# A fused attention and feed-forward kernel: 13 score groups a batch, a ring of exponentials, and one fixed order of all operations

## The chip, the cores and the metric

The kernel runs on one core of one Trainium2 chip. The metric is the time that one execution takes on the device, in microseconds (us); a kernel is run several times and the median is given. TensorE (PE in the profile) does matrix products and transposes, VectorE (DVE) and ScalarE (ACT) do the elementwise work, GpSimd (POOL) and SyncE (SP) mostly start transfers (DMA) here. PSUM is the memory that the results of TensorE go to. An execution is called slow when it lies over 1.5% above the fastest one of the same kernel; verdicts use the fast executions alone.

## The reference

Eight batches of causal attention with 8 heads, 576 queries of 64 numbers and 16 extra keys that every query sees; then three products without a nonlinearity over all 4608 tokens.

```python
k_all = concat([beacon_k, k]); v_all = concat([beacon_v, v])   # 592 keys
scores = q @ k_all.T / sqrt(64)          # causal mask, beacons always seen
a = exp(scores - max); a /= a.sum()
x = (a @ v_all) -> [4608, 512]           # tokens x (heads * 64)
h = (x @ w1) * (x @ w2) @ w3             # 512 -> 1024 -> 1024
out = h @ w_out                          # 1024 -> 512, float32
```

Since nothing stands between w3 and w_out, both kernels multiply the two weights once (Wt = w3 w_out) and use the product. Queries and keys are small, so neither kernel subtracts the maximum.

## The kernel before

It alternates "steps" of attention (64 of them, two to a pair of heads) with matmuls taken from a generator of the feed-forward part. The parts that the change and the argument touch:

```python
GROUPS = [                       # one pair of heads: 4 groups of 368 to 512 columns
    [(1, 112, 128, 0), (0, 0, 240, 128)],
    [(0, 240, 256, 0), (1, 240, 256, 256)], ...]
def scores(s):                   # two 64-row matmuls side by side, one a head
    for g in (2 * half, 2 * half + 1):
        ps = psS.tile([P, 2, 512], FP32, name="ps")        # 2 such pairs in PSUM
        for jt, q0, n, col in GROUPS[g]:
            for hh in range(2):
                nc.tensor.matmul(ps[:, hh, ds(col, n)],
                    kT[ds(hh * 64, 64), t, ts(jt, P)], qT[ds(hh * 64, 64), t, ds(q0, n)])
...
def ff_out(mc, gT):
    ...
        nc.vector.tensor_scalar(ot, pm, float(1.0 / GS), None, ALU.mult)
        nc.sync.dma_start(out[ds(mc * 512 + mt * P, P), :], ot)   # all 36 stores on SyncE
def transpose_qk(b, c):                                           # batches 2 to 7
    nc.sync.dma_start_transpose(qTs[i][:, :, ds(c * P, rows)], q16s[i][:rows, c, :])
    nc.sync.dma_start_transpose(kTs[i][:, :, ds(c * P, P)], k16s[i][:, c, :])
...
def stream():                    # the feed-forward generator
    for mc in range(2): gTs.append((yield from ff_ab(mc)))
    yield from fuse()            # w3 transposed and multiplied by w_out: after two chunks
    ...
for s in range(NSB, NS):         # main loop, from batch 1
    scores(s + 1); exps(s + 1, 0); values(s); emit_ff(k1)
    exps(s + 1, 1); mask(s + 1, 0); emit_ff(fill[s] - k1); mask(s + 1, 1)
    ...
```

The queries and keys of batches 0 and 1 come in large pieces, are cast by VectorE and transposed on TensorE; those of later batches are loaded by GpSimd in pieces of 64 numbers and transposed by DMA from SyncE's queue. So is the attention output x of those batches (x of batches 0 and 1 is transposed on TensorE).

The softmax here doesn't subtract the row's maximum and nothing guards it: scores larger than these inputs give would overflow.

Of the kernel before, what the change touches and what calls it, by code (L numbers as in the profile page):

```python
# [17 lines left out]
GROUPS = [  # L18
    [(1, 112, 128, 0), (0, 0, 240, 128)],
    [(0, 240, 256, 0), (1, 240, 256, 256)],  # L20
    [(3, 368, 128, 0), (2, 240, 256, 128)],
    [(4, 496, 80, 0), (3, 496, 80, 80), (2, 496, 80, 160), (1, 496, 80, 240), (0, 496, 80, 320)],
]
GW = [368, 512, 384, 400]
GO = [400, 768, 1280, 0]
PW = 1664

QT0 = [0, 112, 240, 368, 496]
QTN = [112, 128, 128, 128, 80]
BLK = [  # L30
    [(0, GO[0] + 128)],
    [(0, GO[0] + 240), (1, GO[0])],
    [(0, GO[1]), (1, GO[1] + 256), (2, GO[2] + 128)],
    [(0, GO[1] + 128), (1, GO[1] + 384), (2, GO[2] + 256), (3, GO[2])],
    [(4, 0), (3, 80), (2, 160), (1, 240), (0, 320)],
]
# [3 lines left out]
def kernel(  # L40
# [27 lines left out]
    VS = 72  # L68
    scale = float(D**-0.5)
# [11 lines left out]
    MA = const.tile([P, 240], FP16, name="MA")  # L81
    MB = const.tile([P, 256], FP16, name="MB")
    ident = const.tile([P, P], FP16, name="ident")

    ptp = ctx.enter_context(tc.tile_pool(name="ptp", bufs=2))
    xp = ctx.enter_context(tc.tile_pool(name="xp", bufs=2))
    sm = ctx.enter_context(tc.tile_pool(name="sm", bufs=4))
    gp = ctx.enter_context(tc.tile_pool(name="gp", bufs=2))
    wp = ctx.enter_context(tc.tile_pool(name="wp", bufs=2))
    early = ctx.enter_context(tc.tile_pool(name="early", bufs=8))  # L90
    tiny = ctx.enter_context(tc.tile_pool(name="tiny", bufs=2))
    bkp = ctx.enter_context(tc.tile_pool(name="bkp", bufs=1))
    asb = ctx.enter_context(tc.tile_pool(name="asb", bufs=2))
    op = ctx.enter_context(tc.tile_pool(name="op", bufs=3))
    psS = ctx.enter_context(tc.tile_pool(name="psS", bufs=2, space=bass.MemoryType.PSUM))
    psV = ctx.enter_context(tc.tile_pool(name="psV", bufs=1, space=bass.MemoryType.PSUM))
    psM = ctx.enter_context(tc.tile_pool(name="psM", bufs=3, space=bass.MemoryType.PSUM))

    ctx.enter_context(tc.manual_schedule())


    def load_q(b, c):
        rows = min(P, S - c * P)
        nc.gpsimd.dma_start(  # L104
            q16s[b % NB2][:rows, c, :].rearrange("s (h d) -> s h d", h=H),
            q[b, :, ds(c * P, rows), :].rearrange("h s d -> s h d"),
        )

    def load_kv(b, jt, src, beacon, dst):
        p0 = Nb if jt == 0 else 0  # L110
        s0 = max(0, jt * P - Nb)
        rows = min(P - p0, S - s0)
        nc.gpsimd.dma_start(  # L113
            dst[ds(p0, rows)], src[b, :, ds(s0, rows), :].rearrange("h s d -> s h d")
        )
        if jt == 0:
            nc.gpsimd.dma_start(dst[0:Nb], beacon[b].rearrange("h n d -> n h d"))

    def load_k(b, jt):
        load_kv(b, jt, k, beacon_k, k16s[b % NB2][:, jt, :].rearrange("s (h d) -> s h d", h=H))  # L120

    def load_v(b, jt):
        load_kv(b, jt, v, beacon_v, vas[b % NB2][:, jt, :, 0:64])

    def transpose_qk(b, c):
        i = b % NB2
        rows = min(P, S - c * P)
        nc.sync.dma_start_transpose(qTs[i][:, :, ds(c * P, rows)], q16s[i][:rows, c, :])
        nc.sync.dma_start_transpose(kTs[i][:, :, ds(c * P, P)], k16s[i][:, c, :])


    early_qk, early_b = {}, {}

    def load_pair(b, t):
        for i, src in enumerate((q, k)):
            st = early.tile([P, 2, RUN * D], FP32, name="st")
            if b:
                nc.vector.memset(st[0:1, 0, 0:1], 0.0)
            nc.sync.dma_start(
                st[:NR], src[b, ds(2 * t, 2)].rearrange("h (p j) d -> p h (j d)", j=RUN)  # L140
            )
            early_qk[b, t, i] = st
        if t == 0:
            bst = bkp.tile([Nb, H, D], FP32, name="bst")
            nc.sync.dma_start(bst, beacon_k[b].rearrange("h n d -> n h d"))
            early_b[b] = bst

    o16s = {}

    def cast_pair(b, t):  # L150
        if t == 0:
            b16 = bkp.tile([Nb, DM], FP16, name="b16")
            nc.vector.tensor_copy(b16, early_b[b].rearrange("p h d -> p (h d)"))
            early_b[b] = b16
        o16s[t] = []
        for i in range(2):
            o16 = tiny.tile([P, RUN, P], FP16, name=f"o16_{i}")
            nc.vector.tensor_copy(  # L158
                o16[:NR].rearrange("p j (h d) -> p h j d", h=2),
                early_qk[b, t, i][:NR].rearrange("p h (j d) -> p h j d", j=RUN),  # L160
            )
            o16s[t].append(o16)

    def pe_transpose_pair(b, t):
        qT, kT = qTs[b % NB2], kTs[b % NB2]
        for o16, dst, off, copy in (
            (o16s[t][0], qT, 0, nc.vector.tensor_copy if b or t != 1 else nc.scalar.copy),
            (o16s[t][1], kT, Nb, nc.scalar.copy),
        ):
            pt = psM.tile([P, 1024], FP16, name="pm")  # L170
            for j in range(RUN):
                nc.tensor.transpose(pt[:, ds(j * NR, NR)], o16[:NR, j, :], ident[:NR, :NR])  # L172
            if off:
                nc.tensor.transpose(
                    pt[:, ds(S, Nb)], early_b[b][:, ts(t, P)], ident[:Nb, :Nb]
                )
                copy(dst[:, t, 0:Nb], pt[:, ds(S, Nb)])
            copy(  # L178
                dst[:, t, ds(off, S)].rearrange("p (i j) -> p i j", j=RUN),
                pt[:, 0:S].rearrange("p (j i) -> p i j", j=RUN),  # L180
            )

    def pe_transpose_x(b):
        for i in range(NJT):
            pt = psM.tile([P, NT, P], FP16, name="pm")
            n = QTN[i]
            for t in range(NT):
                nc.tensor.transpose(
                    pt[:, t, 0:n], x16s[b][:n, i, ts(t, P)], ident[:n, :n]
                )  # L190
            dst = xT[:, :, ds(b * S + QT0[i], n)]
            if i % 2:
                nc.scalar.copy(dst, pt[:, :, 0:n])
            else:
                nc.vector.tensor_copy(dst, pt[:, :, 0:n])


    zeros = const.tile([P, 512], FP16, name="zeros")
    nc.vector.memset(zeros, 0.0)  # L199

    def spin(n):
        pm = psM.tile([P, 512], FP32, name="pm")
        for _ in range(n):
            nc.tensor.matmul(pm, zeros[:, 0:P], zeros)  # L204

    nc.vector.memset(ident, 1.0)
    nc.vector.memset(MA, 1.0)
    nc.vector.memset(MB, 1.0)

    def constants(i):  # L210
        nc.vector.memset(kTs[i][:, :, ds(S + Nb, NJT * P - S - Nb)], 0.0)
        nc.vector.memset(vas[i][64:128, 4, :, :], 0.0)
        nc.vector.memset(vas[i][:, 0:4, :, 64:65], 1.0)
        nc.vector.memset(vas[i][0 : S + Nb - 4 * P, 4, :, 64:65], 1.0)

    constants(0)

    for t in range(NT):
        load_pair(0, t)
    nc.gpsimd.affine_select(  # L220
        ident,
        ident,
        pattern=[[1, P]],
        compare_op=ALU.is_equal,
        fill=0.0,
        base=0,
        channel_multiplier=-1,
    )
    for m, base in (
        (MA[:, 0:128], 0),  # L230
        (MA[:, 128:240], Nb),
        (MB[:, 0:128], 0),
        (MB[:, 128:256], 0),
    ):
        nc.gpsimd.affine_select(
            m,
            m,
            pattern=[[1, m.shape[1]]],
            compare_op=ALU.is_ge,
            fill=0.0,  # L240
            base=base,
            channel_multiplier=-1,
        )
    for c in range(NJT):
        load_v(0, c)
    for i in range(NB2):
        nc.gpsimd.memset(k16s[i][64:128, 4, :], 0.0)
        nc.gpsimd.memset(q16s[i][64:128, 4, :], 0.0)
    for c in range(4):
        for i, w in enumerate((moe_w1, moe_w2)):  # L250
            nc.gpsimd.dma_start(
                w12[:, :, ds(i * DF + c * 256, 256)],
                w[:, ts(c, 256)].rearrange("(t p) f -> p t f", p=P),
            )

    def fuse():
        def w3_transposed(kt):
            pt = psM.tile([P, NFT, P], FP16, name="pm")
            for rt in range(NFT):
                nc.tensor.transpose(pt[:, rt, :], w316[:, kt // 2, kt % 2, ts(rt, P)], ident)  # L260
# [295 lines left out]
```

## Time and profile before

| | before |
|---|---|
| time, median of the first 3 runs | 322.3 us (319.26 to 323.62) |
| span of the profiled execution | 316.5 us |
| PE busy | 294.4 us, 93% |
| work of PE at full pace (worked out in the prediction) | 261 us |
| DVE, ACT, POOL busy | 167.1, 158.1, 110.9 us |
| DMA packets under 512 B | 143,104 of 156,960 |

The main lines of the profile stand in the prediction. Two things that the prediction left aside turned out to matter. The first is how long the first pieces of q and k take to land (the view of DMA issues; columns: out<-in, queue, kind, count, KB of one, median us from issue to landing):

```profile
st<-in_q_dram SPq DMA_DIRECT2D x8, 288.0 KB, 7.0
st<-in_k_dram SPq DMA_DIRECT2D x8, 288.0 KB, 7.9
```

The second is what SyncE's queue waits for (the view of that queue's waits; us in total, times, longest):

```profile
SPq L323 <- DVE ot L322: 54.8, 14, 15.1
SPq L323 <- DVE pT L384: 40.0, 10, 15.4
SPq L128 <- DMA q<-in_q_dram: 38.3, 2, 21.7
```

L323 is the output store, and it stands in the same queue as the transposes of q, k and x. The queue takes its entries in order, so while a store waits for a copy, no transpose behind it can start. I had read these lines as harmless, since a queue that waits is not an engine that waits.

### The profile page before, as it was taken

What the parts mean: (1) busy time and instruction counts of PE and PEld (TensorE: products, weight loads), DVE (VectorE), ACT (ScalarE), POOL (GpSimd) and SP (SyncE); (2) the same over time, 40 slices, a digit from 0 to 9 for tenths busy, and PEclk for the clock granted to TensorE, in tenths of its full rate; (3) what the DMA queues carried; (4) which work ended last, traced back from release to release, by engine and by line L of the source; (5) the groups of instructions that cost most, each with busy time, mean ns of one, the idle gap of its engine ahead of it and who ended that gap; (6) DMA issues with size and microseconds to landing.
All of it is one profiled execution on the core that took longest, in us unless ns stands there. A gap on an engine that the chain in (4) does not pass through costs nothing.

```text
span 316.5 us, 7016 instructions
## 1 busy us (share of the span) xinstructions
PE 294.4 (93%) x2826; PEld 151.3 (48%) x2826; DVE 167.1 (53%) x391; ACT 158.1 (50%) x230; POOL 110.9 (35%) x147
## 2 busy tenths in 40 slices
PE   8877688899989999999999999999999999999995
PEld 3445254454545554455544455445554544444442
DVE  4767277455554445555555565555555634344342
ACT  1983466666636554376546645654665231230320
POOL 8954686347756680384067305000000000000000
PEclk9999899999999999999999999999999999999999
DMA  8999999999999999999989999935600330202003
GB/s 188 207 230 284 163 133 143 181 210 175 147 137 152 152 173 189 195 169 175 169 141 126 152 177 169 147 64 133 134 2 33 104 73 35 99 0 99 35 0 133
DMA packets 156960, 42.97 MB, mean 136 GB/s; under 512 B 143104, under 2 KB 151296, under 8 KB 156928
## 3 DMA queue, kind: packets, MB, share of 16 engines
q0 software_dynamic: 102240, 17.28, 75.1%
q1 hardware_dynamic: 54688, 25.25, 42.2%
q8 instruction: 22, 0.36, 0.5%
q14 instruction: 10, 0.08, 0.1%
HBM read 39.32 MB, written 9.44 MB: 154 GB/s over the span
## 4 chain that ended last, share of the span: by engine, by line
PE 78%; DMA 10%; ACT 5%; POOL 4%; DVE 2%; issue 1%; SPq 0%; DVEq 0%
PE pm L291 36%; PE pm L312 18%; PE pv L401 10%; PE ps L363 8%; DMA va<-in_v_dram 5%; PE pm L269 5%; ACT pT L372 2%; DMA qT<-q 2%; DMA w<-in_moe_w_dram 2%; POOL va L113 2%; ACT a_sb L302 2%; PE pm L260 1%; DVE gT L304 1%; ACT kT L178 1%; PE pm L172 1%
## 5 line engine op out<-in xcount | busy, mean ns | idle before, releaser
L291 PE MATMUL pm<-xT,w 128*128 128x512 f16 x576 | 132.6, 382 | 0.0
L372 ACT ACTIVATE pT<-ps 128x736 f16<-128x736 f32 (+3 forms) x128 | 107.0, 869 | 39.2 <-PE ps L363 38.8
L291 PEld LDWEIGHTS <-w 128*128 128x128 f16 x576 | 54.1, 98 | 60.3 <-issue 1.4
L302 ACT ACTIVATE a_sb<-pm 128x512 f32<-128x512 f32 x72 | 43.0, 597 | 79.8 <-PE pm L291 78.8
L304 DVE TENSOR_TENSOR gT<-pm,a_sb 128x512 f16<-128x512 f32 x72 | 49.7, 690 | 46.6 <-PE pm L291 46.1
L312 PE MATMUL pm<-Wt,gT 128*128 128x512 f16 x288 | 65.9, 379 | 0.0
L113 POOL DMA_DIRECT2D va<-in_v_dram x40 | 35.7, 904 | 51.2 <-PE pv L401 27.8
L401 PE MATMUL pv<-va,pT 128*128 128x65 f16 x960 | 40.7, 194 | 5.4 <-DVE x L410 2.2
L363 PE MATMUL ps<-qT,kT 64*128 64x80 f16 (+3 forms) x704 | 37.1, 228 | 7.7 <-ACT pT L372 4.1
L409 DVE RECIPROCAL rd<-pv 128x4 f32<-128x4 f32 x64 | 12.1, 189 | 56.2 <-PE pv L401 56.2
L312 PEld LDWEIGHTS <-gT 128*128 128x128 f16 x288 | 27.1, 98 | 30.4
L401 PEld LDWEIGHTS <-pT 128*128 128x128 f16 x960 | 33.2, 97 | 15.3 <-issue 6.3
L322 DVE TENSOR_SCALAR ot<-pm 128x512 f32<-128x512 f32 x36 | 24.8, 690 | 27.7 <-PE pm L312 24.3
L363 PEld LDWEIGHTS <-kT 64*128 64x128 f16 x704 | 20.7, 94 | 34.2 <-issue 29.9
L410 DVE TENSOR_TENSOR x<-pv,rd 128x256 f16<-128x256 f32 x64 | 31.4, 490 | 2.3
L113 POOL DMA_DIRECT2D k<-in_k_dram x30 | 25.5, 850 | 10.9 <-DMA va<-in_v_dram 5.0
L104 POOL DMA_DIRECT2D q<-in_q_dram x30 | 25.7, 857 | 9.2 <-DMA va<-in_v_dram 2.7
L384 DVE TENSOR_TENSOR pT<-pT,MB 128x512 f16<-128x512 f16 x64 | 19.4, 323 | 0.0
L269 PE MATMUL pm<-wo,wT 128*128 128x512 f16 x64 | 16.4, 380 | 1.0 <-DVE wT L262 1.0
L384 DVE TENSOR_TENSOR pT<-pT,MA 128x480 f16<-128x480 f16 x32 | 12.8, 400 | 0.9 <-ACT pT L372 0.8
L204 PE MATMUL pm<-zeros 128*128 128x512 f16 x26 | 10.0, 492 | 1.3 <-DVE zeros L199 1.3
L158 DVE CAST o<-st 96x768 f16<-96x768 f32 x16 | 10.1, 660 | 1.5 <-DMA st<-in_k_dram 1.2
(43 smaller groups left out, 95.2 us busy)
## 6 DMA issues: line engine op xcount, KB each, us to landing
out_dram<-ot SPq DMA_DIRECT2D x36, 256.0 KB, 2.6
va<-in_v_dram POOLq DMA_DIRECT2D x24, 128.0 KB, 9.0
q<-in_q_dram POOLq DMA_DIRECT2D x24, 128.0 KB, 8.1
st<-in_q_dram SPq DMA_DIRECT2D x8, 288.0 KB, 7.0
st<-in_k_dram SPq DMA_DIRECT2D x8, 288.0 KB, 7.9
k<-in_k_dram POOLq DMA_DIRECT2D x18, 128.0 KB, 9.1
w<-in_moe_w_dram POOLq DMA_DIRECT2D x8, 256.0 KB, 11.0
xT<-in_moe_w_dram POOLq DMA_DIRECT2D x8, 256.0 KB, 10.4
```

Source lines behind the costliest of these rows:

```text
L104: nc.gpsimd.dma_start(q16s[b % NB2][:rows, c, :].rearrange("s (h d) -> s h d", h=H), q[b, :, ds(c * P, rows), :].rearrange("h s d -> s h d"),)
L113: nc.gpsimd.dma_start(dst[ds(p0, rows)], src[b, :, ds(s0, rows), :].rearrange("h s d -> s h d"))
L269: nc.tensor.matmul(pm, wT[:, rt, :], wo16[:, rt, :], start=(rt == 0), stop=(rt == NFT - 1),)
L291: nc.tensor.matmul(pm, w12[:, kt, ds(i * DF + kf * P, P)], xT[:, kt, ds(mc * 512, 512)], start=(kt == 0), stop=(kt == NKT - 1),)
L302: nc.scalar.activation(a_sb, pm, AF.Copy, scale=GS)
L304: nc.vector.tensor_tensor(gT[:, kf, :], pm, a_sb, ALU.mult)
L312: nc.tensor.matmul(pm, gT[:, kf, ts(mt, P)], Wt[:, kf, :], start=(kf == 0), stop=(kf == NFT - 1),)
L363: nc.tensor.matmul(ps[:, hh, ds(col, n)], kT[ds(hh * 64, 64), t, ts(jt, P)], qT[ds(hh * 64, 64), t, ds(q0, n)],)
L372: nc.scalar.activation(pT[:, :, ds(GO[g], GW[g])], pss[s][j][:, :, 0 : GW[g]], AF.Exp, scale=scale)
L384: nc.vector.tensor_tensor(blk, blk, m.unsqueeze(1).to_broadcast([P, 2, n]), ALU.mult)
L401: nc.tensor.matmul(pv[:, 2 * n + hh, 0:65], pT[:, hh, ds(col, P)], va[:, jt, 2 * t + hh, 0:65], start=(jn == 0), stop=(jn == len(BLK[i]) - 1),
L410: nc.vector.tensor_tensor(x16[:, ds(tiles[0], ni), ds(t * P, P)].rearrange("p i (h d) -> p i h d", h=2), pv[:, 0 : 2 * ni, 0:64].rearrange ...
```

## The change

The author's intent: scores in 13 full groups of 512 columns a batch, exponentials in a ring of eight group buffers, value products in two halves a pair of heads, and every operation of every engine placed by one list that was computed beforehand. In the list, `s b g n` is group g of scores of batch b into bank n, `exp`, `m`, `v`, `n` its exponential, mask, value products and division; `lq lk lv` are loads, `Dq Dk TX` DMA transposes, `l3 lo t3 e3 f ew` the product of w3 and w_out, `a b ea eb o eo st` the feed-forward part. The last letter of `st` is the queue of the output store: P is GpSimd, S is SyncE. The list is some 120 lines long; the core of the diff:

```diff
-GROUPS = [ ... ]                        # 4 groups a pair of heads, 368 to 512 columns
+def make_groups(): ...                  # 13 groups a batch, 512 columns each
+ORDER = """
+consts 0; l3 0; lq 0 0; consts 1; spin 10 7; consts 3; lo 0; lk 0 0; lkb 0; l3 1; lq 0 1; lo 1;
+lk 0 1; l3 2; lq 0 2; lo 2; lk 0 2; lq 0 3; consts 2; l3 3; lo 3; lk 0 3; cast 0 0 q; l3 4;
+tq 0 0 6; t3 0 7; eq 0 0 A 6; e3 0 D 7; lq 1 0; castb 0; cast 0 0 k; l3 5; lk 1 0; tk 0 0 5;
+...
+o 0 0 5; ea 1 0 A 6; lq 3 1; o 0 1 6; eo 0 0 A 5; lk 3 1; s 2 0 0;
+s 2 1 2; s 2 2 4; st 0 0 P; eo 0 1 A 6; exp 2 0 0; ...
+"""
-    ptp = ... bufs=2   # pT: [P, 2, 1664]          psS bufs=2, psV bufs=1, psM bufs=3
+    NRING = 8; ring = const.tile([P, NRING, 2, GP], FP16, name="ring")
+    tiles = {0: pair, 6: one_6, 7: one_7}   # banks 2-3 and 4-5: a pair, or two single banks
+    def exp(b, g, n):
+        nc.scalar.activation(held(b, g)[:, :, 0:GW], shape(n, "pair"), AF.Exp, scale=scale)
+    def st(mc, mt, e):
+        queue = nc.gpsimd if e == "P" else nc.sync
+        queue.dma_start(out[ds(mc * 512 + mt * P, P), :], st_of((mc, mt))[:, 0:DM])
-    (generators, main loop)
+    for op in ORDER: ...
```

By the list w3 and w_out are loaded first and multiplied during the start; 28 of 36 output copies go to ScalarE, and 28 of 36 output stores to GpSimd's queue; the filler matmuls at the start fall from 26 to 10.

## The prediction

> **What bounds the kernel now.** I read the page first, then the busy time in stretches of 8 us, the chain that ended last, and the waits.
>
> ```profile
> PE 294.4 (93%) x2826; PEld 151.3 (48%) x2826; DVE 167.1 (53%) x391; ACT 158.1 (50%) x230; POOL 110.9 (35%) x147
> ...
> PE   8877688899989999999999999999999999999995
> ...
> DMA  8999999999999999999989999935600330202003
> ```
>
> TensorE (PE) is the bound, and the other compute engines have room. But the busy share of PE includes the latency of each matmul, so I ask how much of the span its work needs at full pace. The end of the chain gives the pace:
>
> ```profile
> 264.46 6.91 PE pm L312 x32
> 271.37 13.81 PE pm L291 x64
> 285.18 6.91 PE pm L312 x32
> ```
>
> 13.81 us for 64 is 0.216 us for a 512-column matmul, with no hole. The same pace (columns by 2.4 per ns, plus 2.5 ns) for all that PE must do: 864 feed-forward matmuls 186.5 us; the product of w3 and w_out 64 x 0.216 + 64 transposes x 0.056 = 17.4; 960 value products of 65 columns x 0.0296 = 28.4; scores 53,248 columns for two heads side by side, 22.4; transposes of q, k and x 6.4. Sum 261. The span is 316.5; the last matmul starts some 4 us before its end. So 51 us are lost on PE. Where?
>
> ```profile
> 16.00:24.00 8.00, 5.70 (x109) 3.74 (x109) 5.34 (x27) 6.73 (x10) 4.06 (x7) 1.00 1.35 232
> ...
> 32.00:40.00 8.00, 5.15 (x40) 2.46 (x39) 2.19 (x6) 3.18 (x5) 5.47 (x7) 0.80 2.17 157
> ...
> 256.00:264.00 8.00, 8.00 (x39) 3.63 (x37) 3.39 (x5) 2.75 (x5) 0.00 (x0) 1.00 0.05 11
> ```
>
> The columns are PE, weight loads, DVE, ACT, POOL, granted clock, DMA share, GB/s. In the last line PE is full; early on it isn't, while DMA is. The chain says why:
>
> ```profile
> 12.87 7.62 DMA w<-in_moe_w_dram
> 20.77 15.64 DMA va<-in_v_dram
> 36.70 2.79 PE pm L291 x7
> ```
>
> The start waits for loads until 36.7 us. By then PE has done the attention of batch 0 (6.4 us), the q and k transposes of batch 0 and a quarter of batch 1's (2.7), the x transposes of batch 0 (1.0) and a few others (1.3): 11.3 us. So 25 us are lost before 36.7, and 26 after. Of those 26 the waits show the main part:
>
> ```profile
> ACT pT L372 <- PE ps L363: 38.8, 35, 2.5
> PEld L363 <- issue: 29.9, 69, 0.9
> ...
> PE ps L363 <- ACT pT L372: 4.1, 12, 0.6
> ```
>
> At each of 64 runs of score matmuls the weight load of keys stands idle some 0.42 us. From start to start, a matmul before a run of scores takes 0.10 us more than its columns, and the last of a run before the value products 0.18: 0.28 a run, some 13 us in the 48 runs or so after 36.7. Waits of scores for ACT to empty PSUM, and PE transposes that wait for their copies in batch 1, make up most of the rest.
>
> **What the Trainium skill says.** "TensorE: Matmul & The Clock Gate", section "Back-to-back issue gap", gives N/2.4 + 2.5 ns for a warm clock; the trace agrees (216 ns at 512), and not with the 131 ns that the section gives for real streams. The same page, "The mechanism", says that a weight load overlaps matmuls in flight only when their row groups differ. Scores use two 64-row tiles and all else 128 rows; the 0.28 us a run fits that. "What's actually happening" there says that an idle PE falls to half clock; the trace has 0.80 in 32 to 40 us, where PE idled. "DMA: Bandwidth & Descriptors", "Specifications", puts line rate at 512 B and more: here 143,104 of 156,960 packets are smaller, and while loads and DMA transposes run they move at most some 9,000 to 10,000 in 10 us (counted in the packet records).
>
> **The change, part by part.**
>
> *Scores.* 13 groups of 512 columns x 8 batches replace 128 groups of 736 to 1024 elements: the same columns, so PE work stays. ACT: 104 x 1.023 us = 106.4 for 32 x (1.023 + 0.845 + 0.820 + 0.787) = 111.2; 5 us less, off the path. Three PSUM pairs instead of two let two or three groups run together: counting the order, there are 42 runs of scores, some 33 of them after batch 1's values begin, instead of about 48. At 0.28 us that saves 4 us, and most of the 4.1 us of waits for ACT may go.
>
> *Values, masks, outputs.* The values stay 960 matmuls and 64 halves. Masks: 64 with 384 or 768 elements for 96; with some 0.14 us fixed from the rows (160 elements 232 ns, 512 elements 414 ns) about 5 us less on DVE. 28 of 36 output copies and 54 of 72 a_sb copies are on ACT, which comes to some 170 us busy, DVE to some 157. Neither bounds.
>
> *The early order.* This is the large part. w3 and w_out come first, so the 17.4 us of their product, and all q and k transposes of batch 1, fill the start. In the order, PE has 35.7 us of work ahead of the first value products of batch 1 instead of 11.3. But the loads ahead of that point grow too, by w3 and w_out: 6.3 MB read. The eight pieces of w3 landed 1.25 us apart in the trace before (67.0, 68.2, 69.5 us and on), so 10 us, and w_out takes about 5. So v of batch 1, which landed at 38.4, should land at about 52. Those first value products need all five pieces of v. PE's lag there: 52 - 35.7 = 16 us, for 25 before. Gain 9.
>
> *Rest.* Lost after that point: 33 runs x 0.28 = 9; waits for PSUM, the x transposes of batch 1 and a cold clock after the wait 5; late loads 4. That is 18 for 26. Gain 8. The 26 filler matmuls (spins) shrink to 10, in time that waits anyway.
>
> Sum: 261 + 16 + 18 + 4 (tail) = 299 us of span. The median time lies 5.8 above the profiled span (322.3 to 316.5), which gives 305; I lean to 302, because the author could place every operation where the waits allow, and I may have put the late loads and small waits too high.
>
> **Rivals.** (1) *DMA becomes the bound.* A batch has 14,080 small load packets, 7,200 of transposes and some 1,500 others: 22,800, or about 24.5 us at the best rate seen. The order gives PE 22.2 to 25.4 us of work a batch, against a measured 29 us or so now. For it: DMA is at 9 until 180 us. Against: the load queue now idles 12 to 15 us three times (waiting for value buffers), so there is slack. If it loses 3 us in each of six batches, the time is some 315. (2) *The start gains more.* If loads reach the rate that w3 had alone (0.5 MB in 1.25 us), v lands at 46 and the time is near 294. (3) *The w3 product is hidden anyway:* v of batch 1 lands at 60 and the lag stays 25; then only the 8 us of the rest are gained, 311. (4) *A fixed order is brittle:* in-order engines wait for one late copy; six score groups and few PSUM banks then cost some 0.3 us at a time. That is within the range.
>
> **Range and chances.** The start is good to 6 us, DMA to 10 on the slow side, the small waits to 5: 288 to 314. Faster by over 2% means under 315.9, and of the rivals only DMA reaches that: 0.89. Same 0.08, slower 0.03.
>
> **What would show it.** Right: feed-forward starts at about 42 us with the w3 product before it; the first value products of batch 1 near 52 wait for DMA of v; the stretches from 60 to 220 us have PE full with DMA still at 9; pure feed-forward, with no attention, fills the last 69 us (it was 61); busy ACT near 170. Wrong: waits of score matmuls for the DMA transposes of qT or kT in each batch (rival 1), v of batch 1 landing well before 48 or after 57, or ACT, not PE, ending the chain in the attention stage.

## The result

The changed kernel is correct and took 310.05 us (307.89 to 310.8, 4 runs) against 321.21 (319.26 to 323.62, 4 runs) of the kernel before. The ratio is 0.9656, with a 95% interval of 0.958 to 0.973. A ratio here is the mean time of one kernel's fast runs over that of the other's in the same rounds, so not quite the ratio of the medians that are quoted. A second measurement of the unaltered kernel in a later call gave 308.74 us and 0.9643. It is faster by some 11 us; I had predicted 302, within 288 to 314.

The page of the changed kernel, busy times and slices (a digit is the busy share of a fortieth of the span in tenths; PEclk is the granted clock, the share of its full clock at which TensorE may run):

```profile
PE 285.5 (93%) x2842; PEld 152.8 (50%) x2842; DVE 152.8 (50%) x344; ACT 163.1 (53%) x214; POOL 122.2 (40%) x170
...
PE   6697998999999695999999899999999999999994
...
PEclk9999999999999997999999999999999999999999
DMA  7999999999999999998999999999202501202103
```

PE again has holes at the start, and it has new ones in slices 14 and 16 (100 to 108 and 116 to 123 us), which the kernel before did not have. Four stretches of 8 us (columns: PE, weight loads, DVE, ACT, POOL, granted clock, DMA share, GB/s; the DMA share adds up the times of all packets over 16 engines and passes 1 where packets overlap):

```profile
24.00:32.00 8.00, 5.74 (x51) 2.98 (x48) 3.80 (x8) 4.32 (x9) 3.86 (x5) 1.00 1.17 267
...
96.00:104.00 8.00, 5.37 (x55) 2.66 (x53) 4.21 (x9) 3.53 (x5) 3.79 (x5) 1.00 2.00 127
112.00:120.00 8.00, 4.22 (x81) 2.92 (x76) 2.73 (x7) 5.97 (x7) 5.69 (x8) 0.98 2.24 212
120.00:128.00 8.00, 8.00 (x90) 4.77 (x89) 5.61 (x14) 2.54 (x3) 5.08 (x7) 0.81 1.88 150
```

In two of them PE stands for a third to half of the time while the DMA engines are full. The timeline of PE says what it waited for (start, us, operation; in brackets the idle time before it and what ended it):

```profile
104.30 0.35 PE L449 MATMUL pair<-qT,kT 64*128 64x80 f16 x10 [2.93 <-DMA kT<-k]
...
119.80 1.86 PE L521 MATMUL one<-xT,w 128*128 128x512 f16 x4 [3.78 <-DMA xT<-x]
```

Both are DMA transposes that came late. From start to start of the matmuls in the trace's records, less the time that the columns need at the pace of 216 ns for 512, I count six such holes after 100 us: 3.11, 3.96, 0.49, 0.96, 1.12 and 0.56 us, together 10.2 us. The unaltered kernel's second profile has other ones (3.35, 2.67, 0.64, 0.53), together 7.2 us: where they fall varies, that they fall doesn't. A stall can also cost after its end: the granted clock of TensorE stood at 0.5 for 3.4 us from 119.7 us (the 0.81 in the last of the four stretches), and the matmuls of that time took 1.6 us more than at full pace.

At the start the trace shows that v of batch 1 had landed at 53.4 us, as predicted (52). But its first value products began at 57.8 and did not wait for it:

```profile
52.63 5.35 PE L521 MATMUL one<-xT,w 128*128 128x512 f16 x24
57.82 0.53 PE L480 MATMUL one<-va,ring 128*128 128x65 f16 x12
```

The second line has no bracket: no idle time before it. PE was simply behind: the order puts 35.7 us of work ahead of this point, so PE was 57.8 - 35.7 = 22.1 us late. Summed over the matmul records in the same way, PE's lag (the time less the work done) was 10.5 us at 12 us, 13.9 at 20 us and 18.6 at 34 us; in the kernel before it was 9.9, 14.3 and 21.9 at these times. So 14 of the 22 us are lost in the first 20 us, with the old order as with the new one. And the first pieces of q and k land later than before (view of DMA issues, and two lines of the timeline):

```profile
st<-in_q_dram SPq DMA_DIRECT2D x8, 288.0 KB, 13.0
st<-in_k_dram SPq DMA_DIRECT2D x8, 288.0 KB, 13.5
```

```profile
10.27 0.66 PE L391 MATMUL one<-ident,o16k 96*128 96x96 f16 x6 [1.58 <-DVE o16k L383]
...
28.63 0.43 PE L391 MATMUL one<-ident,o16q 96*128 96x96 f16 x6 [1.31 <-DVE o16q L383]
```

In the two lines of the timeline PE waits for o16, the casts of such pieces on VectorE. The last piece of batch 0's k landed at 19.6 us; before it was 13.6. They share the bandwidth with w3 and w_out, 254 to 267 GB/s in these stretches.

The chain that ended last (start, us, what) points there too: where before it went through w1/w2 and v at the start, it now goes through the first piece of w3 (landed at 7.6 us) and then through a piece of q; its end is feed-forward at full pace, as before.

```profile
16.01 15.60 DMA st<-in_q_dram
...
263.85 13.81 PE one L521 x64
277.66 6.91 PE one L542 x32
```

The balance of the two spans: 316.5 - 308.5 = 8.0 us. At the first value products of batch 1 the lag was 36.7 - 11.3 = 25.4 before and is 22.1 after, so by this cut some 3 us come from the start and 5 from what follows.

The cut matters, because the two kernels reach those products at different times and with different work behind them. At equal times the matmul records say something else: at 60 us PE of the changed kernel had done 37.3 us of work against 27.8, a lead of 9.5 us; at 100 us the lead was 13.7, at 124 us, after the two large holes, 5.9, and at the end 8.4. From 60 us on the changed kernel lost 20.1 us and the kernel before 19.0. In this, holes over 0.4 us made up 10.7 for 7.1 us, the slow clock 1.6 for 0, and all that is smaller 7.8 for 11.9; the last is where fewer runs of scores should show. So by this cut the lead is won in the first 60 us, with the early order; after that, what fewer runs seem to give is taken away again by late transposes. (This rests on one profile of each kernel.) The rest of the 11 us is not in the traces: a timed execution takes 1.7 us more than its profiled span (310.18 for 308.5), so the profiled execution of the kernel before took some 318.2, which is below all three of its first timed runs. It was one of its fastest.

SyncE's and GpSimd's queues have changed places:

```profile
SPq L555 <- ACT st L292: 61.2, 8, 39.1
SPq L413 <- DMA q<-in_q_dram: 44.1, 4, 31.9
```

```profile
POOL out_dram L555 <- ACT st L292: 61.9, 19, 25.6
POOL out_dram L555 <- DVE rd L491: 23.6, 6, 9.9
```

On SyncE the 8 store waits are those of the tail, with no transposes behind them; the 28 early ones now stand on GpSimd's queue, 17 of them with loads behind them.

### The profile page after: what moved, and what is told of

Read it like the earlier page. It is cut to its first block, busy times and chain, and to the rows that moved or that the text cites. A ratio compares the mean times of both kernels' runs of the same rounds, so it can differ in the third digit from the quotient of the medians.

```text
span 308.5 us, 7036 instructions
## 1 busy us (share of the span) xinstructions
PE 285.5 (93%) x2842; PEld 152.8 (50%) x2842; DVE 152.8 (50%) x344; ACT 163.1 (53%) x214; POOL 122.2 (40%) x170
## 4 chain that ended last, share of the span: by engine, by line
PE 48%; DMA 22%; issue 14%; POOL 10%; DVE 3%; ACT 2%; POOLq 0%; SPq 0%; DVEq 0%; ACTq 0%
PE one L521 24%; PE one L542 12%; DMA va<-in_v_dram 5%; DMA st<-in_q_dram 5%; PE one L480 4%; PE pair L449 3%; DMA k<-in_k_dram 3%; POOL q L315 3%; PE one L434 3%; DMA xT<-x 2%; POOL k L323 2%; POOL out_dram L555 2%; DMA xT<-in_moe_w_dram 2%; DMA qT<-q 2%; POOL va L323 2%
## 5 line engine op out<-in xcount | busy, mean ns | idle before, releaser
L521 PE MATMUL one<-xT,w 128*128 128x512 f16 x576 | 133.3, 381 | 4.8 <-DMA xT<-x 4.7
L459 ACT ACTIVATE ring<-pair 128x1024 f16<-128x1024 f32 x104 | 98.9, 1030 | 22.5 <-PE pair L449 22.5
L536 DVE TENSOR_TENSOR gT<-one,asb 128x512 f16<-128x512 f32 x72 | 49.7, 691 | 73.3 <-PE one L521 73.3
L542 PE MATMUL one<-Wt,gT 128*128 128x512 f16 x288 | 65.3, 379 | 0.3 <-ACT ring L459 0.2
L292 ACT ACTIVATE asb<-one 128x512 f32<-128x512 f32 x54 | 32.3, 597 | 62.2 <-PE one L521 58.7
L480 PEld LDWEIGHTS <-ring 128*128 128x128 f16 x960 | 34.8, 98 | 11.0 <-issue 3.4
L480 PE MATMUL one<-va,ring 128*128 128x65 f16 x960 | 37.8, 194 | 0.4 <-ACT ring L459 0.3
L449 PE MATMUL pair<-qT,kT 64*128 64x80 f16 (+4 forms) x736 | 32.4, 228 | 5.5 <-DMA kT<-k 3.3
L292 ACT ACTIVATE st<-one 128x512 f32<-128x512 f32 x28 | 16.7, 597 | 37.0 <-PE one L542 37.0
L492 DVE TENSOR_TENSOR x<-one,rd 128x256 f16<-128x256 f32 (+1 forms) x64 | 31.4, 491 | 2.2
L469 DVE TENSOR_TENSOR ring<-ring,MX 128x384 f16<-128x384 f16 x32 | 11.3, 353 | 16.0 <-ACT ring L459 15.9
L469 DVE TENSOR_TENSOR ring<-ring,MD 128x768 f16<-128x768 f16 x32 | 17.6, 550 | 1.8 <-ACT ring L459 1.8
```

Source lines behind the costliest of these rows:

```text
L292: nc.scalar.activation(dst, src, AF.Copy, scale=by)
L449: nc.tensor.matmul(shape(n, "pair")[:, hh, ds(col, w)], kT[ds(hh * 64, 64), t, ts(jt, P)], qT[ds(hh * 64, 64), t, ds(q0, w)],)
L459: nc.scalar.activation(held(b, g)[:, :, 0:GW], shape(n, "pair"), AF.Exp, scale=scale)
L469: nc.vector.tensor_tensor(blk, blk, msk, ALU.mult)
L480: nc.tensor.matmul(pv[:, 2 * at + hh, 0 : D + 1], held(b, g)[:, hh, ds(col, P)], va[:, jt, 2 * t + hh, 0 : D + 1], start=(jt == 0), stop=( ...
L492: nc.vector.tensor_tensor(x16s[b % NB2][:, ds(2 * h, ni), ts(t, P)].rearrange("p i (h d) -> p i h d", h=2), pv[:, 0 : 2 * ni, 0:D].rearran ...
```

## The experiments

My theory after the comparison: (A) less is won at the start because PE follows a chain of pieces, casts, transposes and copies, not v of batch 1; (B) what is won afterwards comes from fewer runs of scores; (C) it is held down by DMA transposes that land late because so many small packets are in flight. Rivals: that the start is limited by the bytes ahead of v; that a change between scores and other matmuls costs nothing by itself and the cost was the wait of weights; that the order of the queues, not the packets, sets when transposes land. Twelve kernels ran, all changed from the changed kernel. The last column is the difference of the ratio to the changed kernel's 0.965 (mean of its two measurements) times 320.5 us; the intervals of two such ratios together leave it uncertain by some 3 us.

| run | median us | ratio to before, 95% | against changed, us |
|---|---|---|---|
| product_late | 313.45 | 0.977 (0.971 to 0.984) | +3.9 |
| switch_each | 317.79 | 0.993 (0.988 to 0.998) | +9.0 |
| same_rows_each | 309.53 | 0.967 (0.962 to 0.972) | +0.7 |
| no_v_after_1 (wrong on purpose) | 304.06 | 0.951 (0.946 to 0.955) | -4.6 |
| w3_one_piece (wrong on purpose) | 304.13 | 0.951 (0.947 to 0.956) | -4.4 |
| batch2_early | 318.62 | 0.995 (0.986 to 1.004) | +9.6 |
| outs_sp | 322.26 | 1.005 (0.996 to 1.014) | +12.8 |
| keys_before_w3 | 308.35 | 0.962 (0.955 to 0.969) | -1.0 |
| after_again (unaltered) | 308.74 | 0.964 (0.959 to 0.970) | -0.2 |
| outs_act | 337.04 | 1.051 (1.045 to 1.057) | +27.5 |
| outs_act_keys | 336.95 | 1.054 (1.047 to 1.060) | +28.4 |
| outs_later | 314.94 | 0.980 (0.975 to 0.985) | +4.8 |

**product_late**: the product of w3 and w_out goes behind the attention of batch 1.

```diff
-l3 0..7, lo 0..3 first; t3, e3, f, ew among the work of batch 0
+l3 0..7, lo 0..3 after "lk 2 4"; t3, e3, f, ew of all r before "o 0 0 5"
-        flat = q16s[i // 2][...]         # wT borrowed the buffers of q
+        return wTs[i]                    # own buffers
```

> The product of w3 and w_out goes back behind batch 1 (its loads after q and k of batch 2), all else as in the changed kernel (308.5 us span, 310 us median, 0.9656 of before). If filling the start with it was what gained (my prediction: PE had 9 us less lag at the first value products of batch 1), PE has 17.4 us less to do in a start that still waits, and the span rises by 8 to 14 us, to some 318, near the time of before. If the loads up to the last batch set the pace wherever the product stands, v of batch 1 lands at about 38 to 40 instead of 53 us, the product is done later in time that would have been lost to late transposes, and the span changes by less than 4 us.

It is 3.9 us slower. Its profile fell in a slow execution (314.9 us of span, mean clock 0.946), so I take only the ratio as firm. That profile has v of batch 1 landed at 41.4 us and its first value products at 45.5; with 17.4 us of product still to do, that compares with 62.9 us for the changed kernel's 57.8. So filling the start with the product is worth some 4 us of time (by the intervals, 1 to 7), not the 9 that my prediction gave to the start. The run moves the product alone; what the early q and k transposes of batch 1 are worth was not tested.

**switch_each** puts a tiny matmul over all 128 rows in front of each of the 104 score groups; **same_rows_each** is its control, the same matmul over 64 rows.

```diff
 def s(b, g, n):
+    nc.tensor.matmul(shape(n, "pair")[:, 0, 0:16], zeros[:, 0:P], zeros[:, 0:16])
 # control: zeros[0:64, 0:P], zeros[0:64, 0:16]
```

> One tiny matmul of 128 rows ahead of each of the 104 score groups, so that every group, and not only each of the 42 runs of groups, leaves and enters the 64-row tiles. By the prediction's 0.28 us a run (0.10 in, 0.18 out) 62 more switches cost some 12 us of PE time (62 x 0.2, as the way out to the next group's own loads is shorter) plus 104 x 0.03 = 3: span 318 to 326 if PE sets the pace, some 3 to 6 us if half of it disappears in waits for DMA. If a switch costs nothing and the idle weight load is only waiting that lies elsewhere, the span rises by 3 us or less.

> The control of the run with 128 rows: the same 104 tiny matmuls, but of 64 rows like the scores, so no switch between tile shapes is added. If the switch costs (8.8 us more than the changed kernel was the whole), this one costs 104 x 0.03 = 3 us or less, 1 us after what waits absorb. If it is any added weight load and matmul that costs, it is as slow as that run: 7 to 9 us more.

The 128-row matmul costs 9.0 us and the 64-row one nothing that can be measured (0.7, inside the intervals). So it is the change of rows, not the number of matmuls. The list has 42 runs of scores; 104 need 62 changes more each way. From start to start the trace of switch_each shows 0.093 us over the columns for a change out of scores and 0.107 for one into them (medians), 62 x 0.20 = 12 us gross, of which 9 arrive at the end: PE then waits less for late transposes (holes over 0.4 us after 60 us: 4.2 us for 10.7). Net, that is 9.0 / 62 = 0.145 us a run. The change has 22 runs fewer than the kernel before (42 for 64), so that part is worth some 3.2 us net (an estimate from this run).

**no_v_after_1** does not load v after batch 1, **w3_one_piece** loads only the first of eight pieces of w3. Both give wrong results on purpose; they take bytes and packets away without moving anything.

```diff
 def lv(b, c):
+    if b > 1: return          # and in lvb       (no_v_after_1)
 def l3(r):
+    if r: return              # t3 reads piece 0 each time   (w3_one_piece)
```

> Wrong result on purpose: v of batches 2 to 7 is not loaded (batches 0 and 1 are used again), 28,400 of 154,000 packets less, no instruction of a compute engine less. If the rate of small packets makes the transposes of q, k and x late, the six stalls of PE after 100 us (3.1 + 4.0 + 0.5 + 1.0 + 1.1 + 0.6 = 10 us) and the slow clock after the second go, and the span falls to 296 to 300. If the stalls come from the order in which the transposes are issued behind each other, they stay: 305 or more.

> Wrong result on purpose: one of the eight pieces of w3 is loaded and used eight times, 3.7 MB of 11 MB less to read by 32 us, the same work on every compute engine. If the bytes read set the pace of the start (some 370 GB/s), v of batch 1 lands at about 43 instead of 53 us, the lag of PE by 60 us falls from 22.6 to some 14, and the span falls by 8 to 12 us, to about 298, as all later loads come 10 us sooner too. If the chains of small copies and transposes set the start, the lag falls by less than 3 us, though the later loads still come sooner: 303 to 307.

Without v the time falls by 4.6 us. The large holes at 101 and 116 us are gone, but the scores still wait once for queries at 127.4 to 130.1 (2.67 us). So these loads do make transposes late, and removing them wins about half of the 10 us. Whether by their packets or by their place in GpSimd's queue the run can't say, since it removes both. For w3 it is the same gain, and for a reason that I had not seen: v of batch 1 landed at 46.5, seven us sooner, and PE came to its value products at 56.3 for 57.8, only 1.5 sooner. The landing of v doesn't set the start. Nor does that of q and k explain it alone: their pieces also came faster than in the changed kernel,

```profile
st<-in_q_dram SPq DMA_DIRECT2D x8, 288.0 KB, 9.5
```

and the last one at 30.5 us instead of 35.3, but its transpose started at 37.1 instead of 38.5. (The first eight landed at nearly the same times in both, until 18.6 and 19.6 us, so the run says nothing of the first 20 us.) The other 3 us came later, probably because all later loads were ahead of schedule; its waits of PE have a single late transpose:

```profile
PE pair L453 <- DMA qT<-q: 3.1, 1, 3.1
PE one L430 <- DMA xT<-in_moe_w_dram: 2.3, 1, 2.3
PE one L395 <- DVE o16k L387: 1.8, 1, 1.8
```

**keys_before_w3** moves the first keys ahead of the first piece of w3 on VectorE, TensorE and ScalarE, to shorten the chain at the start.

```diff
-cast 0 0 q; tq 0 0 6; t3 0 7; eq 0 0 A 6; e3 0 D 7; castb 0; cast 0 0 k; tk 0 0 5; ek 0 0 A 5
+cast 0 0 q; cast 0 0 k; castb 0; tq 0 0 6; eq 0 0 A 6; tk 0 0 5; ek 0 0 A 5; t3 0 7; e3 0 D 7
```

> In the first 10 us the cast of the first keys stands on DVE behind the copy of the first transposed piece of w3, which lands at 7.6 us. It is moved ahead of it, with its PE transposes and copies. If in-order chains of small operations set the start (the run with one piece of w3: v of batch 1 landed 7 us sooner, PE came there only 1.5 us sooner), the lag at the first value products of batch 1 (57.8 us) falls by about 2 us and the span by 1 to 2. If loads set it: no change, within 0.5 us.

It is 1.0 us faster, within the interval of 7 thousandths each way: nothing is shown. Its profile fell in a slow execution, so I don't explain by it. Its longest wait of PE at the start is another one (for w_out, 2.7 us); that would fit a chain whose links all come about as late as each other, but it is not shown.

**batch2_early** sends q and k of batch 2 the way of batches 0 and 1: large pieces, casts, transposes on TensorE. That takes 9,216 small load packets (576 rows, 8 heads, q and k) and 10 DMA transposes away.

```diff
-Dq 2 *, Dk 2 *; lq 2 4, lk 2 4
+castb 2; cast 2 t q; cast 2 t k; tq 2 t; tk 2 t; eq 2 t A; ek 2 t D   (t = 0..3, among batch 1)
-        if b < 2:   # lq, lkb: large pieces
+        if b < 3:
```

> q and k of batch 2 come as those of batches 0 and 1 do: packets of 1,536 bytes, a cast on DVE and transposes on PE, for 9,344 small load packets and some 4,600 packets of transposes. PE gets 104 - 52 = 52 more small transposes, about 2.4 us, DVE and ACT some 10 us, all in the time of batch 1. If the small packets make later transposes late, everything that DMA does after 60 us comes some 8 us sooner, the six stalls after 100 us (10 us) mostly go, and the span falls by 4 to 8 us in sum, to 300 to 305. If the stalls come from the order of issue, only the added PE work is left: 310 to 312.

It is 9.6 us slower, which neither side of the expectation had, though the packets are gone; late transposes still cost 8.3 us in holes after 100 us, for 10.2. VectorE had no room for the casts between 64 and 77 us (PE waited 1.65, 1.04 and 2.15 us there), and most loads of batch 3 came later (the queries after the first output store at 86.9 us, in the changed kernel at 77.7), because GpSimd's queue stood still (its timeline; the idle time in brackets):

```profile
68.04 0.88 POOL L327 DMA_DIRECT2D k<-in_k_dram  x1
85.84 0.58 POOL L559 DMA_DIRECT2D out_dram<-st  x1 [16.91 <-ACT st L296]
86.92 0.89 POOL L319 DMA_DIRECT2D q<-in_q_dram  x1 [0.49 <-issue]
```

The first output store waits 16.9 us for its copy, and most loads of batch 3 stand behind it. This is where the third rival, the order of the queues, came up; the following runs are about it.

**outs_sp** puts the 28 stores back on SyncE's queue, where the kernel before had them.

```diff
-st 0 0 P ... st 6 3 P
+st 0 0 S ... st 6 3 S
```

> The 28 output stores that the change issues from GpSimd go to the queue of SyncE as in the kernel before. GpSimd waits 89 us for outputs in the changed kernel, and loads stand behind those waits. If that holds loads back, the loads come sooner and the span falls by 2 to 5 us. If the stores then stand in the way of the transposes on SyncE, stalls of PE on qT, kT and xT grow: 2 to 6 us more. Within 2 us: the two balance.

It is 12.8 us slower: the whole gain is gone. SyncE's waits and what PE waits for:

```profile
SPq L557 <- ACT st L294: 71.5, 17, 15.2
```

```profile
PE pair L451 <- DMA qT<-q: 7.1, 2, 6.6
PE pair L451 <- DMA kT<-k: 5.4, 2, 3.1
PE one L523 <- DMA xT<-x: 4.2, 1, 4.2
```

The 28 stores wait for their copies in front of the transposes, and PE waits 16.7 us for transposes, for 9.1 in the changed kernel by the same view. The rest is the clock: it stood at 0.5 for 6.8 us from 164.1 and again from 198.2 us, at the two longest of these waits, and by the matmul records the slow clock cost 5.8 us of PE's time, for 1.6 in the changed kernel. One must not read this as "12.8 of the 11 us": the list was made for stores on GpSimd. But in this list the one letter decides over as much time as the whole change gains.

**outs_act** and **outs_act_keys**: then the stores should be better still where neither transposes nor loads stand behind them. ScalarE makes 28 of the 36 copies itself, so they went to its queue; the second run adds keys_before_w3. The unaltered kernel ran beside them.

```diff
-queue = nc.gpsimd if e == "P" else nc.sync
+queue = {"P": nc.gpsimd, "A": nc.scalar}.get(e, nc.sync)      # and "P" -> "A" in the list
```

> The changed kernel unaltered, as the yardstick of this call: ratio 0.96 to 0.973, some 309 to 311 us.

> The 28 output stores that the changed kernel issues on GpSimd's queue are issued on ScalarE's, which also makes most of the copies that they wait for; no other place in the order changes. Theory 'in-order queues': outputs then stand ahead of neither the transposes (SyncE) nor the loads of q, k and v (GpSimd, which stood 61.9 and 23.6 us at outputs by the waits of the changed kernel), so loads start earlier and the stalls for late transposes shrink from 10 us to under 5: 303 to 307 us, ratio 0.94 to 0.955. Rival 'rate of small packets': the loads are limited by the packets that the engines move, not by when they are issued, so nothing changes: 308 to 311 us. Second rival: ScalarE stands at stores of copies that VectorE made, exponentials come late, and it is slower: over 312 us.

> Both edits: output stores on ScalarE's queue, and the first keys cast and transposed ahead of the first piece of w3. If the two are independent: outs_act less the 1 us of keys_before_w3, some 302 to 307 us by the first theory, and a version that beats both kernels; by the rival 307 to 311 us.

Both are slower by some 28 us: the side of my second rival, but much further. ScalarE's own timeline shows the first store:

```profile
76.22 0.60 ACT L294 ACTIVATE st<-one 128x512 f32<-128x512 f32 x1 [1.07 <-PE one L544]
86.24 0.39 ACTq L557 DMA_DIRECT2D out_dram<-st  x1
86.74 0.60 ACT L294 ACTIVATE st<-one 128x512 f32<-128x512 f32 x1 [9.92 <-DMA qT<-q]
```

The copy was done at 76.8, and the store followed 9.4 us later. It did not wait for VectorE, as my rival had it, but for a DMA transpose of q. The trace's records say why: every transfer raises a counter when it lands, and in this program the transfers of SyncE and of ScalarE share eight counters in turn, those of GpSimd have eight others. All 28 stores on ScalarE start after the last transfer on their counter has landed, and in the attention stage that is, but for one, a transpose of SyncE's (for the first store one issued 7 us before). Nine of the 28 start 0.076 to 0.077 us after that landing (86.24 after 86.16, 130.96 after 130.88, 204.36 after 204.28, ...). While ScalarE stands there, no exponential and no copy moves, and PE stands 8.7 us (to 87.4 us) and 8.3 us (to 132.4) at once. The pair with the other edit came out the same, so the two edits add up to nothing here.

**outs_later** leaves the stores on GpSimd's queue, but each one that has loads to come stands eight loads later in it.

```diff
-st 0 0 P; ... lk 3 1; ...          # in its place
+... ; st 0 0 P                      # behind the next eight of lq, lk, lkb, lv, lvb; so 17 of the 28
```

> The output stores stay on GpSimd's queue, but each of those issued while loads are still to come stands behind the next eight loads in that queue; nothing else changes, and no other engine waits for a store sooner. In the changed kernel this queue stood still 9.95 us (to 178.3) and 6.4 us (to 205.5) at a store whose copy was not ready, with loads behind it. Theory 'loads stand behind stores': loads start up to 10 us earlier, transposes land in time, the stalls after 100 us (10.2 us) shrink to 4 to 7: 303 to 307 us, ratio 0.945 to 0.957. Rival 'rate of packets and free buffers': the loads of v wait for buffers that TensorE frees and the rest for the engines that move packets, so it stays at 308 to 311 us. Slower (over 312) if loads that start earlier delay the transposes of x and q that are due first.

It is 4.8 us slower. This is the last case of the expectation (slower), and its reason fits: beside loads that start earlier, the transposes take longer. PE's timeline:

```profile
118.22 1.86 PE L523 MATMUL one<-xT,w 128*128 128x512 f16 x4 [5.05 <-DMA xT<-x]
...
165.50 1.37 PE L451 MATMUL pair<-qT,kT 64*128 64x80 f16 x20 [5.10 <-DMA qT<-q]
```

The transpose of x that the first line waits for was issued at 109.4 and landed at 118.0, 8.6 us later; five loads of v went out just before and beside it. In the changed kernel it was issued at 113.0 and landed at 119.6, after 6.6 us. Even so PE goes on 1.6 us sooner here than there (118.22 for 119.80); what makes the run slower comes at the second line, where the transpose took 9.3 us (156.0 to 165.4), for 6.2 in the changed kernel (155.5 to 161.7). The holes over 0.4 us after 60 us are only 0.8 us longer in sum (11.5 for 10.7), but the clock stood at 0.5 for 6.8 us at each of the two, which cost 5.4 us for 1.6. So a store in front of loads also holds them back while transposes pass, and here that seems to help. None of my versions beats the changed kernel beyond the intervals.

## Why the prediction was right or wrong

The direction, the range and the main idea held: 310.05 lies within 288 to 314, TensorE stays the bound, and the gain comes from holes in its work. The central figure was 8 us too low, and a wrong offset hid a part of the error (below). By its own steps:

- **The start, "PE's lag there: 52 - 35.7 = 16 us, for 25 before. Gain 9".** This step failed. The landing at 52 was right (53.4, which is also what its terms 38.4 + 10 + 5 add up to). But the lag was 22.1 us and the gain some 3. The step took it that PE is late only because v is late, and so that 35.7 us of work ahead could be done by then. The first half is shown to be wrong: PE did not wait for v, and in w3_one_piece v seven us sooner moved PE by 1.5 us. So is the second: at 52 us PE had done 30 us of work, and had lost 14 us by 20 us. Why is open in part. This work needs q and k, and the same w3 and w_out that were moved ahead of v were also moved beside q and k: their pieces took 13.0 us instead of 7.0 to land. But in w3_one_piece they took 9.5, which moved PE no more than the 1.5 us. The chain of casts, transposes and copies that each piece goes through in turn is argued from the waits; keys_before_w3, which shortened one link, did not show it.
- **Rest, "That is 18 for 26. Gain 8".** In the trace the losses after the start are 308.5 - 261 - 22.1 - 4 = 21.4 us, so the gain is 5. The term that was too small is "late loads 4": 10.2 us by the trace, and 1.6 more for the slow clock after the longest of them. The other terms, "33 runs x 0.28 = 9" and 5, came to some 10 together.
- **The switch of rows, "At 0.28 us that saves 4 us".** Right as a mechanism: switch_each and its control separate it from the number of matmuls. But 0.28 is too much: the 0.18 for the way out seems to count half of the last matmul's columns as loss. Whole runs of scores take 0.20 us over their columns in both kernels (0.10 in, 0.09 out), and the counts were off too (54 runs after 36.7 us in the kernel before, not 48; 31 after 57.8 us in the changed one, not 33). For 22 runs fewer in all, 0.145 net a run makes 3.2 us and 0.20 gross 4.4, so the 4 us came out by luck.
- **"The median time lies 5.8 above the profiled span".** Wrong: it is 1.7. The profiled execution of the kernel before was among its fastest. By itself this made the prediction 4 us too high, which was luck: without it the figure would have been 12 us too low. My lean from 305 to 302, "the author could place every operation where the waits allow", took 3 off without evidence.
- **Sum.** The span was to be 299 and is 308.5: 6 more at the start, 3.4 in the rest. With 4.1 less for the offset and the lean of 3 taken back this gives the 8 us.
- **Engines.** ACT 163.1 us for "some 170", DVE 152.8 for 157; neither bounds. The last 69 us without attention came as predicted (236 to 304). Feed-forward began at 52.7 instead of 42, which is the start again.
- **Rival 1, "DMA becomes the bound"**, is partly true: scores and x do wait for late transposes, 7 to 10 us in all, as its sign said. But not by 3 us in each of six batches. no_v_after_1, which takes 28,400 packets and their places in the queue away, gets half of it back, and batch2_early, with 9,216 packets fewer, almost nothing. Its sign "in each batch" did not occur. Rivals 2 and 3 did not come about: v landed near 53, not 46 or 60. Rival 4, waits for one late copy, stayed small in the changed kernel (PE waited 1.3 us for exponentials); outs_act shows how large they can become.
- **What I did not see at all** is the queue of the stores. I counted the copies of the outputs that move to ACT and passed over the `P` at the end of `st`. The profile before had it: SyncE's queue stood 94.8 us at output stores (a part of it in the tail), and transposes stood behind them. In outs_sp, going back costs 12.8 us. How much of the 11 us it makes in the step from the old loop is open: there the same queue had other work behind its stores, and the parts are not additive (product 3.9, runs 3.2 and stores 12.8 are together more than 11, and the late transposes overlap with each).

## What to carry to other kernels

When loads are moved ahead of a wait, ask not only when the awaited tile lands, but what else lands later for it, and whether the work that is meant to fill the time needs just that. Look at which transfers share an in-order queue with the ones that TensorE waits for, since a store that waits for its copy holds up everything behind it, and look at what the store itself must wait for before choosing another queue. Count a stall of TensorE with what follows it: here the slow clock cost up to 3.0 us a time, and in outs_later it added more than the stalls themselves. Judge the distance from profile to median from more than one execution.

## What the Trainium skill lacked or had wrong

- "DMA: Bandwidth & Descriptors", section "Issuing engines are not separate DMA queues", says that starting transfers from several engines only saves time on the sequencer. For bandwidth no run here speaks against it. For time it is incomplete: the same 28 stores gave 309 us on GpSimd's queue, 322 on SyncE's and 337 on ScalarE's, because of what stands behind a store that waits.
- On no page that I read: that transfers issued by SyncE and by ScalarE may share a set of completion counters, so that one waits for the other. Nine of 28 stores here started 0.077 us after the landing of a transpose from the other queue. This is how this program was built, not shown to be a property of the chip.
- "TensorE: Matmul & The Clock Gate", "The mechanism", says when a weight load overlaps, and "TensorEngine Tiling (Array Packing)", "Key Properties", that a change of tiling mode (how many rows of its array a matmul takes) drains TensorE; neither gives the cost of going between 64-row and 128-row matmuls. Here it is 0.20 us for a run of scores, some 0.10 us each way, and none for a matmul over the same rows.
- "TensorE: Matmul & The Clock Gate", "Back-to-back issue gap": N/2.4 + 2.5 ns agrees with the 13.81 us for 64 matmuls (216 ns each) of the changed kernel as well; the 131 ns for real streams appears in neither.
- "DMA: Bandwidth & Descriptors", "DMA Transpose (X-bar)", gives no time for a transpose beside loads. By the view of the queries' transposes in the changed kernel:

```profile
DMA to landing us min/median/max: 2.4/6.4/10.9
```

The transpose with the minimum was issued at 210.0 us, behind the last load, the one with the maximum at 89.3 us, among loads; whoever places such a transpose in a fixed order among loads like these must leave some 11 us, not 2.4.
